# Value products of a cycle over all 512 queries in one PSUM bank, the output job in the other bank

## The chip, the cores and the metric

The kernel runs on one core of one Trainium2 chip. The metric is the device time of one execution in microseconds (us); the kernel before takes 912.35 us, the median of three runs (912.16 to 912.91). Engines are called by the names of the profile: PE is the tensor engine's matrix products and PEld its weight loads, DVE the vector engine, ACT the scalar engine, POOL GpSimd, SP the engine that issues most DMAs.

## The reference, cut to what matters

One attention block and one MLP block read the same x of 2048 tokens by 448 features, and a sigmoid gate per token mixes their results.

```python
q = (x @ wq) in 16 heads of 28;  k = x @ wk;  v = x @ wv      # one key head and one value head for all
p = softmax(q k^T * 28 ** -0.5)
a = (p v of all heads, side by side) @ wo
b = x1 + gelu(layernorm(x1) @ w3) @ w4
out = g * a + (1 - g) * b
```

All is float32. The change lies in `p v`, which the kernel computes together with the scores and the product with `wo`.

## The kernel before, in words

Two stages come first, in the first 400 us of the span: the projections and the token mixing, then the MLP. The third stage is the attention, and all that the change touches is in it. It works through 16 units of 512 queries by 4 heads, and in each unit through 16 tiles of 128 keys. **A cycle** (the loop over `c`, 128 of them, 8 to a unit) takes two key tiles.

PSUM has eight banks of 128 partitions by 512 floats: four `singles` and two `pairs` of two. In cycle `c` the names `s0, s1, s2, s3_` are the four singles, and they change places from cycle to cycle: the banks that are `s0, s1` in one cycle are `s2, s3_` in the next. `pairs[0]` and `pairs[1]` keep their places (after the first cycle, `pair_1` and `pair_0` in the program's own names).

The order of all five engines' instructions is the order in which the code is written, since the schedule is manual. In a cycle the code writes:

1. `score_tiles` (L205) for the first key tile: the transposed scores of four heads, one bank each, in `s0`, `s1` and the two banks of `pairs[0]`. These are three rounds of four products (keys as weights, 32 rows of the array each), and a bank holds its scores after its third product.
2. `exps` (L258) on ACT: the exponential of `s0`, then of `s1`, from PSUM into the tile `p` in SBUF. DVE copies `pairs[0]` into `p` as it is (L953), and ACT does its exponential later, in place.
3. `score_tiles` for the second key tile in `s2`, `s3_` and `pairs[1]`, and `exps` of `s2`, of `s3_`, of `pairs[1]`, and of the copied part of the first tile.
4. `values` (L892): the products of the **preceding** cycle's two `p` tiles with the values. `vext` holds a column of ones beside the 28 value columns, so one product also gives the softmax's sum. Heads stand side by side in the array (32 columns each), and each product is recorded as two. Before the change this is done in two halves of 256 queries: the first half in the left half of `s0`, the second in the left half of `s1`.
5. `values_end` (L813 in a unit's first cycle, L817 in all others) on DVE: adds what stands in PSUM to the unit's sum `o`, once for each half.
6. `run_jobs` or its two parts `job_products` (PE, L843) and `job_adds` (DVE, L859, in the first cycles L878): one **output job**, 224 output columns of 128 tokens of an earlier unit times `wo` (in the first cycles times `w4`), in the right half of `s0`. From cycle 11 on every cycle has a job; before, the odd ones from 3.
7. In the third cycle of a unit (`MAX_AT`), for all units but the last: `max_part` between the two halves, which takes the maxima of the next unit's scores over 16 keys. PE writes them in `pairs[0][:, 0]` (L212), DVE reduces them (L219). There are 15 such cycles. In the last unit a second job stands at that place.

So four banks are used twice in a cycle's length: by a cycle's scores, and by values and job after ACT has read the scores. `s0` and `s1` of a cycle are written next by the second key tile's scores of the next cycle, after DVE has read values and job out of them.

Of the kernel before, what the change touches and what calls it, by code (L numbers as in the profile page):

```python
# [42 lines left out]
def gated_mix_kernel(  # L43
# [152 lines left out]
    def q_low(u):  # L196
        nc.vector.tensor_sub(ql_of[u], qr_of.pop(u), f32(qh_of[u]))
# [24 lines left out]
    def max_part(u, ts, ps):  # L222
        max_products(u, ts, ps)
        max_reduce(u, ts, ps)
# [32 lines left out]
    def exps(p, heads, source=None):  # L257
        nc.scalar.activation(p[:, heads], p[:, heads] if source is None else source, AF.Exp, scale=SCALE)  # L258
# [4 lines left out]
    with tc.tile_pool(name="s1b", bufs=1) as s1b, \  # L263
            tc.tile_pool(name="ps1", bufs=1, space=PSUM) as ps1:
        s1_stack = ExitStack()
        s1 = s1_stack.enter_context(tc.tile_pool(name="s1", bufs=1))
# [55 lines left out]
        def first_queries():  # L322
            ps = [mm1(f"q_{g}") for g in range(NG)]
            ah, al = xact[0]
            cols = [slice(g * P, (g + 1) * P) for g in range(NG)]
            for g in range(NG):
                nc.tensor.matmul(ps[g], wqraw[:, 0, cols[g]], xraw[0][:, 0, :], start=True, stop=False)
            for c in range(1, 4):
                for w, a in ((wqh, ah), (wqh, al), (wql, ah)) if c < 3 else ((wqh, ah), (wql, ah)):
                    for g in range(NG):  # L330
                        nc.tensor.matmul(ps[g], w[:, c, cols[g]], a[:, c, :], start=False, stop=(c == 3 and w is wql))
            return ps
# [160 lines left out]
        q0 = first_queries()  # L493
# [275 lines left out]
    with tc.tile_pool(name="s3", bufs=1, reuse_waits="tile") as s3, \  # L769
# [15 lines left out]
        def q_fetch(u):  # L785
            if u < NU:
                q_load(u, qr)

        def q_begin(u):
            q_high(u, s3.tile([P, 512], F32R, tag="qh", bufs=3, name=f"qh_{u}"),  # L790
                   s3.tile([P, 512], F32R, tag="ql", bufs=3, name=f"ql_{u}"))
# [15 lines left out]
        def values_end(u, pv, qs=slice(0, 512)):  # L807
            if u not in o_of:
                o_of[u] = s3.tile([P, 512], F32, tag="o", bufs=2, name=f"o_{u}")
                fresh.add(u)  # L810
            o = o_of[u][:, qs]
            if u in fresh:
                nc.vector.tensor_copy(o, pv)  # L813
                if qs.stop == 512:
                    fresh.remove(u)
            else:
                nc.vector.tensor_add(o, o, pv)  # L817

        def sums_begin(u):
            o = o_of.pop(u)  # L820
            rt = s3.tile([P, 16], F32, tag="rt", bufs=2, name=f"rt_{u}")
            nc.sync.dma_start(rt, o[0:128:32, :].rearrange("j (a b) -> j a b", b=16))
            return u, o, rt

        def recip(u, o, rt, checked=True):
            rr = s3.tile([P, 16], F32, tag="rr", bufs=2, name=f"rr_{u}")
            nc.vector.reciprocal(rr, rt)
            if checked:
                check(rr.rearrange("p (a b) -> p a b", b=4), 0)
            rd = dram.tile([4, 512], F32, tag="rd", bufs=2, name=f"rd_{u}")  # L830
            nc.sync.dma_start(rd.rearrange("j (a b) -> (j a) b", b=16), rr)
            rb = s3.tile([P, 512], F32, tag="rb", bufs=2, name=f"rb_{u}")
            nc.sync.dma_start(rb, rd.unsqueeze(1).broadcast_to([4, 32, 512]))
            return u, o, rb

        def norm(u, o, rb):
            on_of[u] = s3.tile([P, 512], F32, tag="on", bufs=2, name=f"on_{u}")
            nc.vector.tensor_mul(on_of[u], o, rb)
# [44 lines left out]
        def score_tiles(u, kt, first, second, third, fourth):  # L883
            scores(u, kt, [first, second, third, fourth])
            p_of[u * NT + kt] = p = s3.tile([P, 4, 512], F32, tag="p", bufs=PB, name=f"p_{u}_{kt}")
            return p

        def values(ks, pv, qs=slice(0, 512)):
            for k in ks:
                u, kt = divmod(k, NT)  # L890
                for j in range(4):
                    nc.tensor.matmul(pv[32 * j:32 * j + 32, :], vext[:, kt, :], p_of[k][:, j, qs],  # L892
                                     start=(k == ks[0]), stop=(k == ks[-1]), tile_position=(0, 32 * j))
                if qs.stop == 512:
                    p_of.pop(k)
# [7 lines left out]
        def job_products(ps, n):  # L903
            adds = []
            for _ in range(min(n, len(jobs))):
                products, add, args, cols = jobs.pop(0)
                part = ps[:, 0:D // 2] if n == 1 else ps[:, cols]
                products(*args, part, cols)
                adds.append((add, args, part, cols))
            return adds  # L910

        def job_adds(adds):
            for add, args, part, cols in adds:
                add(*args, part, cols)

        def run_jobs(ps, n):
            job_adds(job_products(ps, n))
# [3 lines left out]
        IDLE = range(2, 12, 2)  # L921
        HINTS = {8 * NT // 2 + 4: [mybir.EngineType.SP],
                 14 * NT // 2 - 2: [mybir.EngineType.DVE, mybir.EngineType.Activation]}
        for c in range(NC):
            u, i = divmod(c, NT // 2)
            k = 2 * c
            s0, s1, s2, s3_ = singles if c % 2 == 0 else singles[2:] + singles[:2]
            if c == 0:
                pb = score_tiles(u, 1, s2, s3_, s0, s1)
                for j, ps in enumerate((s2, s3_, s0, s1)):  # L930
                    exps(pb, slice(j, j + 1), ps.unsqueeze(1))
                pa = score_tiles(u, 2, *(q[:, h] for q in pairs for h in range(2)))
                nc.vector.tensor_copy(pa[:, front], pairs[0])
                for ps, n in zip((s2, s3_), JOBS_0):
                    run_jobs(ps, n)
                exps(pa, both, pairs[1])
                exps(pa, front)
                pairs.reverse()
                continue
            if c > 1:  # L940
                pa = score_tiles(u, 2 * i, s0, s1, pairs[0][:, 0], pairs[0][:, 1])
                with tc.block() if c in HINTS else nullcontext():
                    if c in HINTS:
                        tc.mark_branch_hint_location("redo", "LikelyTaken", HINTS[c])
                    exps(pa, left, s0.unsqueeze(1))
                exps(pa, right, s1.unsqueeze(1))
            if i == 2 and u == 0:
                q_begin(1)
            if i == 3 and u == 0:
                q_low(1)  # L950
                q_fetch(2)
            if 1 < c < NC - 1:
                nc.vector.tensor_copy(pa[:, both], pairs[0])  # L953
            elif c > 1:
                exps(pa, both, pairs[0])
            if i == 3 and later:
                later.pop(0)()
            if i == 1 and sums:
                norms.append(recip(*sums.pop()))
            if i == (3 if u == NU - 1 else 4) and norms:  # L960
                w = norms[0][0]
                norm(*norms.pop())
            if i == 5 and u + 2 < NU:
                q_begin(u + 2)
            if i == 6 and u + 2 < NU:
                q_low(u + 2)
                q_fetch(u + 3)
            pb = score_tiles(u, 2 * i + 1, s2, s3_, pairs[1][:, 0], pairs[1][:, 1])
            exps(pb, left, s2.unsqueeze(1))
            exps(pb, right, s3_.unsqueeze(1))  # L970
            exps(pb, both, pairs[1])
            if 1 < c < NC - 1:
                exps(pa, both)
            if u and i == (3 if u == NU - 1 else 4):
                jobs += [(wo_products, wo_add, (u - 1, t), cols) for t in range(4) for cols in halves]
            v = (c - 1) // (NT // 2)
            at_max = i == MAX_AT and u + 1 < NU
            q0, q1 = slice(0, 256), slice(256, 512)
            values((k - 2, k - 1), s0[:, q0], q0)
            values_end(v, s0[:, q0], q0)  # L980
            if at_max:
                max_part(u + 1, range(4), pairs[0][:, 0])
                later.append(lambda u=u: max_end(u + 1))
            elif i == MAX_AT:
                run_jobs(pairs[0][:, 0], 1)
            values((k - 2, k - 1), s1[:, q0], q1)
            adds = job_products(s0[:, q1], 0 if c in IDLE or c == 1 else 1)
            values_end(v, s1[:, q0], q1)
            job_adds(adds)
            if i == 0 and v < NU - 1:  # L990
                sums.append(sums_begin(v))
        assert not sums and not norms and not later and len(jobs) == 3
# [151 lines left out]
```

## Time and profile before

| what | before |
|---|---|
| median of 3 runs | 912.35 us |
| the profiled execution: its time, its span | 912.95 us, 911.2 us |
| PE busy | 904.7 us (99%) |
| ACT busy | 633.1 us (69%) |
| DVE busy | 517.1 us (57%) |
| granted TensorE clock, mean of the span | 1.000 |
| DMA, mean over the span | 52 GB/s |

The span runs from the first to the last instruction of the program; the execution's own time has 1.75 us more. Matrix products are pipelined: a product's record lasts longer than it keeps the next one waiting, and records of the four heads lie on one another. So PE's busy share says that something was always under way and not that no time is lost. In the views by time a row is a start, a duration, the engine, the line, the operation, out<-in by the program's names with their shape, a count, and in brackets the idle time of the engine before it with what ended it.

### The profile page before, as it was taken

To read this page: it belongs to the slowest core of one execution; us is meant where nothing else is said; L and a number is where in the kernel's file an instruction comes from. 1 tells how busy PE (TensorE), PEld (TensorE's weight loads), DVE (VectorE), ACT (ScalarE), POOL (GpSimd) and SP (SyncE) were. 2 spreads that over 40 slices of the span, in tenths; PEclk is the share of its full clock that TensorE was granted. 3 is DMA by queue.
4 is the path that set the end of the run, shared out by engine and by line. 5 is a ranking of instruction groups with operands and counts; after the bars stand their busy time and mean duration, and the time that the engine had idled before them with its cause. 6 is when DMAs were issued, how large, how long until landed. Compare 5 with 4: busy or idle time off the path is not lost.

```text
span 911.2 us, 24150 instructions
## 1 busy us (share of the span) xinstructions
PE 904.7 (99%) x10360; PEld 627.6 (69%) x10360; DVE 517.1 (57%) x961; ACT 633.1 (69%) x1003; POOL 78.3 (9%) x116
## 2 busy tenths in 40 slices
PE   9999999999999999999999999999999999999998
PEld 6788888888888888875555555555555555555554
DVE  4665273631431531136766776776767667767665
ACT  5442344332131231269999999999999999999995
POOL 3243330200000520020000000000000000000000
PEclk9999999999999999999999999999999999999999
DMA  8832654120110020010000001000011000010001
GB/s 306 282 97 54 150 168 131 32 75 1 35 53 2 18 69 1 1 52 24 14 25 14 24 15 55 23 25 17 24 33 36 25 14 25 15 55 13 15 14 44
DMA packets 40582, 47.31 MB, mean 52 GB/s; under 512 B 10136, under 2 KB 28632, under 8 KB 40472
## 3 DMA queue, kind: packets, MB, share of 16 engines
q1 hardware_dynamic: 37304, 40.30, 15.1%
q10 hardware_dynamic: 3168, 5.44, 1.6%
q8 instruction: 82, 1.34, 0.6%
q14 instruction: 28, 0.23, 0.1%
HBM read 32.56 MB, written 11.67 MB: 49 GB/s over the span
## 4 chain that ended last, share of the span: by engine, by line
PE 98%; ACT 2%; DVE 0%; issue 0%
PE bank L892 26%; PE bank L205 19%; PE bank L843 6%; PE acc L700 5%; PE acc L698 5%; PE acc L699 5%; PE g L137 4%; PE g L138 4%; PE g L136 4%; PE pair L205 3%; ACT p L258 2%; PE hs L474 1%; PE hs L475 1%; PE g L139 1%; PE g L140 1%; PE h L137 1%
## 5 line engine op out<-in xcount | busy, mean ns | idle before, releaser
L258 ACT ACTIVATE p<-bank 128x512 f32<-128x512 f32 x514 | 266.1, 605 | 4.7 <-POOL pick L865 1.5
L892 PE MATMUL bank<-p,vext 128*32 128x256 f32 x4064 | 247.7, 382 | 1.0 <-ACT p L258 0.8
L892 PEld LDWEIGHTS bank<-p,vext 128*32 128x32 f32 x4064 | 118.0, 110 | 115.8 <-ACT p L258 53.0
L953 DVE COPY p<-pair 128x1024 f32<-128x1024 f32 x125 | 153.1, 1225 | 57.2 <-PE pair L205 33.0
L688 ACT ACTIVATE gh<-g 128x512 fp32r<-128x512 f32 x55 | 32.9, 598 | 182.8 <-PE g L140 182.8
L817 DVE TENSOR_TENSOR o<-o,bank 128x256 f32<-128x256 f32 x222 | 93.6, 421 | 81.4 <-PE bank L892 70.3
L258 ACT ACTIVATE p<-p 128x1024 f32<-128x1024 f32 x126 | 138.0, 1095 | 0.0
L258 ACT ACTIVATE p<-pair 128x1024 f32<-128x1024 f32 x129 | 136.7, 1060 | 0.0
L690 DVE TENSOR_TENSOR gl<-gf,gh 128x512 fp32r<-128x512 f32 x55 | 38.5, 699 | 165.8 <-ACT gf L689 165.8
L205 PE MATMUL bank<-qh,kh 32*128 32x512 f32 x514 | 115.2, 444 | 0.1
L205 PE MATMUL pair<-qh,kh 32*128 32x512 f32 x510 | 114.1, 444 | 0.0
L205 PE MATMUL bank<-qh,kl 32*128 32x512 f32 x514 | 102.0, 389 | 0.0
L205 PE MATMUL bank<-ql,kh 32*128 32x512 f32 x514 | 101.8, 390 | 0.0
L205 PE MATMUL pair<-qh,kl 32*128 32x512 f32 x510 | 101.1, 389 | 0.0
L205 PE MATMUL pair<-ql,kh 32*128 32x512 f32 x510 | 100.7, 390 | 0.0
L205 PEld LDWEIGHTS bank<-qh,kh 32*128 32x128 f32 x514 | 48.0, 182 | 62.0 <-issue 38.7
L700 PE MATMUL acc<-w4h,gl 128*128 128x448 f32 x220 | 80.7, 367 | 0.0
L698 PE MATMUL acc<-w4h,gh 128*128 128x448 f32 x220 | 80.2, 365 | 0.0
L699 PE MATMUL acc<-w4l,gh 128*128 128x448 f32 x220 | 79.9, 363 | 0.0
L843 PE MATMUL bank<-wof,on 128*32 128x224 f32 (+1 forms) x984 | 69.5, 357 | 0.0
L136 PE MATMUL g<-ah,w3h 128*128 128x512 f32 x168 | 65.5, 390 | 0.0
L137 PE MATMUL g<-al,w3h 128*128 128x512 f32 x168 | 65.4, 390 | 0.0
(207 smaller groups left out, 1397.5 us busy)
## 6 DMA issues: line engine op xcount, KB each, us to landing
qd<-qf ACTq DMA_DIRECT2D x15, 256.0 KB
rb<-rd SPq DMA_DIRECT2D x15, 256.0 KB
x<-in_x_dram SPq DMA_DIRECT2D x4, 896.0 KB
xd<-xt SPq DMA_DIRECT2D x16, 224.0 KB
w34raw<-in_w_dram SPq DMA_DIRECT2D x7, 512.0 KB
qr<-qd SPq DMA_DIRECT2D x64, 56.0 KB
w34raw<-in_w_dram SPq DMA_DIRECT2D x7, 448.0 KB
out_dram<-ot SPq DMA_DIRECT2D x14, 224.0 KB
```

Of the source, the lines that this page charges most:

```text
L136: nc.tensor.matmul(ps, wh[:, c, :], ah[:, c, :], start=(c == 0), stop=False)
L137: nc.tensor.matmul(ps, wh[:, c, :], al[:, c, :], start=False, stop=False)
L205: nc.tensor.matmul(ps[j], k[h, keys], q[h, :], start=(r == 0), stop=(r == 2), tile_position=(32 * j, 0))
L258: nc.scalar.activation(p[:, heads], p[:, heads] if source is None else source, AF.Exp, scale=SCALE)
L690: nc.vector.tensor_sub(gl, gf, f32(gh))
L698: nc.tensor.matmul(ps, gh[:, tok], w4h[i][:, k, :], start=(f == 0), stop=False)
L699: nc.tensor.matmul(ps, gh[:, tok], w4l[i][:, k, :], start=False, stop=False)
L700: nc.tensor.matmul(ps, gl[:, tok], w4h[i][:, k, :], start=False, stop=(f == stop))
L817: nc.vector.tensor_add(o, o, pv)
L843: nc.tensor.matmul(ps[32 * i:32 * i + 32, :], a[:, c:c + 32], w, start=start, stop=stop, tile_position=(0, 32 * i))
L892: nc.tensor.matmul(pv[32 * j:32 * j + 32, :], vext[:, kt, :], p_of[k][:, j, qs], start=(k == ks[0]), stop=(k == ks[-1]), tile_position=(0, ...
L953: nc.vector.tensor_copy(pa[:, both], pairs[0])
```

## The change

```diff
-            q0, q1 = slice(0, 256), slice(256, 512)
-            values((k - 2, k - 1), s0[:, q0], q0)
-            values_end(v, s0[:, q0], q0)
+            values((k - 2, k - 1), s0)
+            values_end(v, s0)
             if at_max:
                 max_part(u + 1, range(4), pairs[0][:, 0])
                 later.append(lambda u=u: max_end(u + 1))
             elif i == MAX_AT:
                 run_jobs(pairs[0][:, 0], 1)
-            values((k - 2, k - 1), s1[:, q0], q1)
-            adds = job_products(s0[:, q1], 0 if c in IDLE or c == 1 else 1)
-            values_end(v, s1[:, q0], q1)
-            job_adds(adds)
+            run_jobs(s1, 0 if c in IDLE or c == 1 else 1)
```

All 512 queries' value products go to `s0` in products of 512 columns, half as many as before; DVE adds them to `o` in one instruction of 512 columns; the job's products go to the left of `s1`; the maxima stand behind all of the value products. `values` and `values_end` have 512 queries as their default. Lines behind the change are numbered 4 lower in the changed kernel.

PE, the end of a cycle in the 13th unit, before. `bank_0` and `bank_1` are `s0` and `s1` here, `p_...` the exponentials; a row stands for one instruction or several of the same kind (x3, x4), and in brackets are the engines whose semaphores it waits for:

```order
L892 MATMUL bank_0_3209<-p_12_10_9579,vext_78 32x256 [waits Activation_49]
L892 MATMUL bank_0_3209<-p_12_10_9579,vext_78 32x256 x3
L892 MATMUL bank_0_3209<-p_12_11_9598,vext_78 32x256 x4
L892 MATMUL bank_1_3210<-p_12_10_9579,vext_78 32x256 [waits Activation_49]
L892 MATMUL bank_1_3210<-p_12_10_9579,vext_78 32x256 x3
L892 MATMUL bank_1_3210<-p_12_11_9598,vext_78 32x256 x4
L843 MATMUL bank_0_3209<-wof_3256,on_11_9525 32x224 [waits DVE_49]
L843 MATMUL bank_0_3209<-wof_3256,on_11_9525 32x224 x3
L205 MATMUL bank_2_3211<-qh_12_8583,kh_1048 128x512 [waits Activation_49]
```

The same place on PE in the changed kernel:

```order
L892 MATMUL bank_0_3209<-p_12_10_8679,vext_78 32x512 [waits Activation_49]
L892 MATMUL bank_0_3209<-p_12_10_8679,vext_78 32x512 x3
L892 MATMUL bank_0_3209<-p_12_11_8698,vext_78 32x512 x4
L843 MATMUL bank_1_3210<-wof_3256,on_11_8634 32x224 [waits Activation_49]
L843 MATMUL bank_1_3210<-wof_3256,on_11_8634 32x224 x3
L205 MATMUL bank_2_3211<-qh_12_7827,kh_1048 128x512 [waits Activation_49]
```

Sixteen products of 256 columns became eight of 512, and the job's wait for DVE became one for ACT.

PE, the second key tile's scores of the cycle after that, before; these are the next writers of `bank_0` and `bank_1`:

```order
L205 MATMUL bank_0_3209<-qh_12_8583,kh_1048 128x512 [waits DVE_49]
L205 MATMUL bank_1_3210<-qh_12_8583,kh_1048 128x512
L205 MATMUL pair_0_3258<-qh_12_8583,kh_1048 128x512 [waits Activation_49]
L205 MATMUL pair_0_3258<-qh_12_8583,kh_1048 128x512
L205 MATMUL bank_0_3209<-ql_12_8584,kh_1048 128x512
```

The same place on PE in the changed kernel:

```order
L205 MATMUL bank_0_3209<-qh_12_7827,kh_1048 128x512 [waits DVE_49]
L205 MATMUL bank_1_3210<-qh_12_7827,kh_1048 128x512 [waits DVE_49]
L205 MATMUL pair_0_3258<-qh_12_7827,kh_1048 128x512 [waits Activation_49]
L205 MATMUL pair_0_3258<-qh_12_7827,kh_1048 128x512
L205 MATMUL bank_0_3209<-ql_12_7828,kh_1048 128x512
```

The last reader of these banks on DVE, the job's add, read `bank_0` before and reads `bank_1` now, so the wait for it moved from the first product of the four to the second.

DVE, a cycle with maxima in the 14th unit, before; `mr_14` takes the maxima of the next unit out of `pair_1`:

```order
L953 COPY p_13_4_9881<-pair_1_3259 128x1024 [waits PE_49]
L817 TENSOR_TENSOR o_13_9852<-o_13_9852,bank_0_3209 128x256 [waits DVE_49,PE_49,Activation_49]
L219 TENSOR_REDUCE mr_14_9927<-pair_1_3259 128x4x4 [waits PE_49]
L817 TENSOR_TENSOR o_13_9852<-o_13_9852,bank_1_3210 128x256 [waits DVE_49,PE_49,Activation_49]
L859 SCALAR_TENSOR_TENSOR ot_11_8438<-bank_0_3209,gg_79,ot_11_8438 128x224 [waits PE_49]
```

The same place on DVE in the changed kernel:

```order
L953 COPY p_13_4_8936<-pair_1_3259 128x1024 [waits PE_49]
L817 TENSOR_TENSOR o_13_8916<-o_13_8916,bank_0_3209 128x512 [waits DVE_49,PE_49,Activation_49]
L219 TENSOR_REDUCE mr_14_8982<-pair_1_3259 128x4x4 [waits PE_49]
L859 SCALAR_TENSOR_TENSOR ot_11_7700<-bank_1_3210,gg_79,ot_11_7700 128x224 [waits PE_49,Activation_49]
L953 COPY p_13_6_9001<-pair_1_3259 128x1024 [waits PE_49]
```

The reduction stood behind the add of the first half and ahead of that of the second; now it stands behind the add of all 512 queries.

## The prediction

> **What bounds the kernel now.** The page first, to see which engines could be the bound; then the attention stage by itself in the view of windows, as the page's shares are a mean over three stages.
>
> ```profile
> PE 904.7 (99%) x10360; PEld 627.6 (69%) x10360; DVE 517.1 (57%) x961; ACT 633.1 (69%) x1003; POOL 78.3 (9%) x116
> 600.00:700.00 100.00, 100.00 (x1696) 56.73 (x1688) 70.98 (x136) 99.70 (x154) 0.00 (x0) 1.00 0.08 26
> ```
>
> In the 100 us from 600 to 700 PE is busy for 100.00 and ACT for 99.70, at a clock of 1.00; DVE has 29 us to spare. A busy share doesn't tell which of the two sets the pace, so the timeline of one cycle is next: weight loads, then DVE and ACT, then two rows of products.
>
> ```profile
> 603.07 1.45 PEld L892 LDWEIGHTS bank<-p,vext 128*32 128x32 f32 x32 [0.42 <-ACT p L258]
> 605.32 0.18 PEld L205 LDWEIGHTS bank<-qh,kh 32*128 32x128 f32 x2 [0.36 <-issue]
> 605.97 0.19 PEld L205 LDWEIGHTS bank<-qh,kh 32*128 32x128 f32 x2
> 606.96 1.45 PEld L892 LDWEIGHTS bank<-p,vext 128*32 128x32 f32 x32 [0.42 <-ACT p L258]
> 605.13 0.42 DVE L817 TENSOR_TENSOR o<-o,bank 128x256 f32<-128x256 f32 x1 [0.44 <-PE bank L892]
> 605.47 0.45 DVE L859 SCALAR_TENSOR_TENSOR ot<-bank,gg,ot 128x224 f32<-128x224 f32 x1
> 606.31 2.07 ACT L258 ACTIVATE p<-bank 128x512 f32<-128x512 f32 x4
> 606.59 0.38 PE L205 MATMUL pair<-qh,kl 32*128 32x512 f32 x1
> ```
>
> I count from the first value product (603.07). The next cycle's value products start at 606.96, so **a cycle takes 3.89**. The first key tile's scores start at 2.25, the second's at 2.90, the last score product at 3.52. The exponential of `s0` starts at 3.24, and the values, which overwrite `s0`, wait for its end (the bracket). On DVE the second half's add starts at 2.06, the job's add at 2.40, ending at 2.85. Then comes the row that matters: the second tile's scores load weights at 2.90, 0.05 after the job's add. They write the bank that this add reads, so **they already stand right behind DVE**.
>
> That ACT isn't the floor shows in the first cycles, which have a job only every other time (ACT's first exponential of three successive cycles):
>
> ```profile
> 415.13 2.07 ACT L258 ACTIVATE p<-bank 128x512 f32<-128x512 f32 x4
> 418.90 2.10 ACT L258 ACTIVATE p<-bank 128x512 f32<-128x512 f32 x4
> 422.83 2.06 ACT L258 ACTIVATE p<-bank 128x512 f32<-128x512 f32 x4
> ```
>
> 3.77 without a job, 3.93 with one: ACT can do 3.77 and is held to 3.89 by the loop through PE. So up to 0.12 a cycle could be won, and every delay of PE's loop is paid.
>
> One cycle of this execution shows that loop with DVE late (PEld, DVE, PE):
>
> ```profile
> 559.74 1.45 PEld L892 LDWEIGHTS bank<-p,vext 128*32 128x32 f32 x32 [0.41 <-ACT p L258]
> 562.18 0.42 DVE L813 COPY o<-bank 128x256 f32<-128x256 f32 x1 [0.81 <-PE bank L843]
> 562.52 0.44 DVE L859 SCALAR_TENSOR_TENSOR ot<-bank,gg,ot 128x224 f32<-128x224 f32 x1
> 563.02 0.18 PEld L205 LDWEIGHTS bank<-qh,kh 32*128 32x128 f32 x2 [0.49 <-DVE ot L859]
> 563.60 0.41 PE L205 MATMUL pair<-qh,kl 32*128 32x512 f32 x2
> 563.93 0.16 PEld L892 LDWEIGHTS bank<-p,vext 128*32 128x32 f32 x8 [0.37 <-ACT p L258]
> ```
>
> Here DVE's add came 0.38 later than usual (2.44). The job's add ended at 3.22, the scores' weights followed at 3.28 with DVE named as releaser, and the values 0.91 behind them: 4.19, which is 0.30 longer than usual. In such a cycle ACT's exponential is long done. The price is nearly the delay itself, because there was next to no slack.
>
> **The change, part by part.**
>
> *Value products.* Sixteen of 256 columns become eight of 512. What a column costs, from rows of two widths: the last group of four at 256 is followed by the next group 0.22 later, groups of 448 follow each other in 0.38.
>
> ```profile
> 608.50 0.40 PE L892 MATMUL bank<-p,vext 128*32 128x256 f32 x4
> 608.72 0.56 PE L843 MATMUL bank<-wof,on 128*32 128x224 f32 x8
> 903.98 0.56 PE L843 MATMUL bank<-wof,on 128*32 128x448 f32 x4
> 904.36 0.56 PE L843 MATMUL bank<-wof,on 128*32 128x448 f32 x4
> ```
>
> That is 0.86 and 0.85 ns a column, the same within the rounding: nothing to win by width, at most 0.01 a cycle, and the values end where they ended. TensorE: Matmul & The Clock Gate of the Trainium skill, section Back-to-back issue gap, gives 81 ns for a sustained product of 128 columns and 131 ns for one of 512, less than half per column; by an estimate from these two, value products would shrink by far more than the whole 0.12 that ACT leaves open. The rows above show no such saving.
>
> *The job.* It no longer waits for DVE. That wait (18.5 us of PEld in all, its row is with the rivals) hid behind products: the job's first one (608.72) follows the values' last group (608.50) in a group's usual 0.22. Worth nothing.
>
> *The add.* One instruction in place of two. Rows for its length (DVE, by operation and shape):
>
> ```profile
> L817 DVE TENSOR_TENSOR o<-o,bank 128x256 f32<-128x256 f32 x222 | 93.6, 421 | 81.4 <-PE bank L892 70.3 <-ACT p L258 7.3 <-issue 2.7
> L764 DVE TENSOR_TENSOR x<-x,acc 128x448 f32<-128x448 f32 x4 | 2.4, 622 | 7.2 <-PE acc L700 7.2
> L838 DVE TENSOR_TENSOR on<-o,rb 128x512 f32<-128x512 f32 x15 | 10.2, 681 | 0.0
> ```
>
> 421 ns at 256 and 622 at 448 make 1.047 ns a column, so 0.69 at 512; below stands 0.68 (no operand in PSUM), above twice 0.42. DVE saves time in sum. But before, half of it was done while PE was still at the second half; only 0.42 lay behind the last product. Now all 0.69 does.
>
> *The loop.* The add starts at 2.05. The next instruction on DVE starts 0.08 before an add's end (605.13 + 0.42 against 605.47): the job's add at 2.66, ending at 3.11. Its bank is now `s1`, so the second product of the second tile's scores waits for it, and all behind that one: weights at 3.16. Values 0.91 behind, as in the late cycle: 4.07. **Against 3.89 that is 0.18 a cycle.** Ends: 4.02 if the loads of the other heads, made meanwhile, save the array's filling; 4.12 with the usual cycle's 0.99 between these weights and the values (2.90 to 3.89). Cycles with a job and scores behind it, none of the dear kind below and not the late one: 101 from 11 to 126, and 3, 5, 7, 9: 105. **18.9 us**, ends 13.7 and 24.2. The cycles without a job have ACT's 3.77 as their floor, and the single add frees `s0` at 2.74; I cost them at nothing.
>
> *Cycles with maxima.* Rows of one (PE, DVE, PEld):
>
> ```profile
> 626.42 1.07 PE L892 MATMUL bank<-p,vext 128*32 128x256 f32 x16
> 627.30 0.30 PE L212 MATMUL pair<-khd,qh 128*32 128x64 bf16 x16
> 627.95 0.42 DVE L219 TENSOR_REDUCE mr<-pair 128x16 f32<-128x256 f32 x1
> 628.78 0.19 PEld L205 LDWEIGHTS bank<-qh,kh 32*128 32x128 f32 x2 [0.36 <-ACT p L258]
> 630.43 0.59 PEld L892 LDWEIGHTS bank<-p,vext 128*32 128x32 f32 x16 [0.42 <-ACT p L258]
> ```
>
> 4.01 a cycle, 0.12 above the others for the extra products. The reduction ends at 1.95, and the next cycle's first scores, which write the same pair, load at 2.36: 0.41 of cover. In the changed order the reduction stands behind the long add: 2.66 to 3.08. The third product of the **first** key tile's scores waits for it, to 3.13, and everything on PE behind. From those scores to the values PE alone needs 1.27 (605.32 to 606.59) and 0.33 (563.60 to 563.93), 1.60 in all: 4.73, 0.72 more. Ends: 4.53, if the two heads that don't wait run ahead and only ACT counts, and 4.77 with the usual 1.64 (605.32 to 606.96). The last unit's extra job, DVE's 0.45 on the same pair, I cost alike: 16 cycles, **11.5 us**, ends 8.3 and 12.2.
>
> *The sum:* 18.9 + 11.5 = 30.4 us on the profiled execution's 912.95 (span 911.2 and 1.75 around it): 943.3. That execution lies 0.60 above the median of the runs, so I predict **942.7 us**; by the ends 934.4 to 948.8.
>
> **The rivals.**
>
> *Freed products (faster).* One mechanism: the value products and the job get through PE earlier, because wide products are cheaper and no job waits for an add. It decides only if PE gives back time that DVE's longer add doesn't take, over 0.18 a cycle. ACT's 3.77 is then the floor: 105 x 0.12 = 12.6 us, 899.8. For it: the weight loads of the job did wait.
>
> ```profile
> L843 PEld LDWEIGHTS bank<-wof,on 128*32 128x32 f32 x896 | 24.1, 108 | 24.3 <-DVE o L817 18.5 <-DVE o L813 3.3
> ```
>
> Those are 21.8 us of waits for DVE from 450 to 890 us. Against it: the products' rows without a gap, and the same price per column. PSUM — Partial Sum Buffer of the Trainium skill, section PSUM bank collisions raise a hardware error, wants two engines kept apart by whole bank and 32 partitions, not by address; by that rule the old job had to wait for the add of the other columns, and the trace agrees (18.5 us). The page doesn't say that such a wait costs time.
>
> *Cover in ordinary cycles.* The second tile's scores have more slack than the late cycle shows, so that only cycles with maxima pay: 912.35 + 11.5 = 923.9. Against it: 0.05 from add to weights in the usual cycle, and 0.30 lost for 0.38.
>
> *The change does nothing.* Both waits are taken up by a slack in ACT that I don't see: 912. Against it: 3.89 is already above ACT's 3.77.
>
> *A dearer add.* If 512 columns take twice 0.42, the loop grows by 0.15 more in all 121 cycles: 18.2 us, 960.9. Against it: 622 ns at 448.
>
> **How the numbers follow.** Forecast 0.82; cover in ordinary cycles 0.07; dearer add 0.05; freed products 0.03; nothing 0.03. 912.35 within 0.2% (1.8 us) is about what a measurement can't tell from no change. Faster 0.03, same 0.03, slower 0.94. The range takes in the ends and a little for what the 0.05 steps between engines may do: 932 to 951; cover, freed products, nothing and the dearer add lie outside with 0.18.
>
> **What would show it.** In the changed profile: values starting 4.07 apart in ordinary cycles and 4.7 in those with maxima; the weight loads of the second tile's scores waiting for DVE's job add, some 0.3 each time; the third load of the first tile's scores waiting for the reduction in 15 cycles; ACT's share from 600 to 700 us falling from 99.7 to about 93; the 512-column add at 0.69. The prediction is wrong if those loads wait no longer than now, if the values end earlier than 1.9 after their start, or if ACT stays at 99.7.

## The result and the profile after

The changed kernel takes **941.5 us**, the median of four runs (940.93 to 942.86), against 912.3 us before (also four runs by now): a ratio of 1.0319 with a 95% interval of 1.0307 to 1.0331. The profiled execution took 941.43 us, its span is 939.6 us, so the profiled executions differ by 28.5 us and their spans by 28.4 us.

The page's first part, and the window from 600 to 700 us of the changed kernel:

```profile
PE 929.0 (99%) x8328; PEld 583.4 (62%) x8328; DVE 499.9 (53%) x834; ACT 636.3 (68%) x1003; POOL 79.9 (8%) x116
600.00:700.00 100.00, 99.17 (x1213) 45.48 (x1209) 63.98 (x104) 94.79 (x145) 0.00 (x0) 1.00 0.07 22
```

DVE has 17 us less to do and PEld 44 us, and the kernel is 29 us slower. In the window DVE's share fell from 71 to 64 and so did ACT's, from 99.7 to 94.8: ACT, which was nearly full, now waits. PE still reads 99, since a product's record lasts longer than it keeps the next one waiting (0.40 against 0.22 in the prediction's rows at 608.50 and 608.72); a busy share of PE wouldn't have shown the loss.

An ordinary cycle, weight loads first, then DVE and ACT:

```profile
626.57 0.16 PEld L892 LDWEIGHTS bank<-p,vext 128*32 128x32 f32 x8 [0.36 <-ACT p L258]
628.80 0.18 PEld L205 LDWEIGHTS bank<-qh,kh 32*128 32x128 f32 x2 [0.36 <-ACT p L258]
629.37 0.18 PEld L205 LDWEIGHTS bank<-qh,kh 32*128 32x128 f32 x1
629.72 0.18 PEld L205 LDWEIGHTS bank<-qh,kh 32*128 32x128 f32 x1 [0.17 <-DVE ot L859]
630.62 0.16 PEld L892 LDWEIGHTS bank<-p,vext 128*32 128x32 f32 x8 [0.37 <-ACT p L258]
628.62 0.69 DVE L817 TENSOR_TENSOR o<-o,bank 128x512 f32<-128x512 f32 x1 [1.58 <-PE bank L892]
629.22 0.45 DVE L859 SCALAR_TENSOR_TENSOR ot<-bank,gg,ot 128x224 f32<-128x224 f32 x1
629.80 1.58 ACT L258 ACTIVATE p<-bank 128x512 f32<-128x512 f32 x3
```

Counted from the first value product, the add starts at 2.05 and the job's add at 2.65; it ends at 3.10. The first of the second tile's loads is made at 2.80 and the next only at 3.15, 0.05 behind the job's add, with DVE named in the bracket. The values follow 0.90 later: the cycle is 4.05 long. The last load's bracket names ACT, but ACT's exponential of `s0` started at 629.80 and takes 0.6, so it was done at 630.40, 0.22 ahead. What the values wait for is PE's own scores in front of them: the last of these start at 630.29, 0.33 ahead, as far as in the late cycle of the prediction. That is the sign that PE's loop is no longer held by ACT, as it was before.

A cycle with maxima:

```profile
638.74 0.16 PEld L892 LDWEIGHTS bank<-p,vext 128*32 128x32 f32 x8 [0.37 <-ACT p L258]
641.09 0.18 PEld L205 LDWEIGHTS bank<-qh,kh 32*128 32x128 f32 x2 [0.36 <-ACT p L258]
641.86 0.18 PEld L205 LDWEIGHTS pair<-qh,kh 32*128 32x128 f32 x2 [0.59 <-DVE mr L219]
643.46 0.16 PEld L892 LDWEIGHTS bank<-p,vext 128*32 128x32 f32 x8 [0.36 <-ACT p L258]
640.79 0.69 DVE L817 TENSOR_TENSOR o<-o,bank 128x512 f32<-128x512 f32 x1 [1.59 <-PE bank L892]
641.39 0.42 DVE L219 TENSOR_REDUCE mr<-pair 128x16 f32<-128x256 f32 x1
642.66 1.09 ACT L258 ACTIVATE p<-bank 128x512 f32<-128x512 f32 x2 [0.84 <-PE bank L205]
```

The first two heads of the first tile's scores load at 2.35, the other two at 3.12, behind the reduction that stands behind the long add. ACT idles 0.84 for scores. The cycle is 4.72 long.

The view of waits from 450 us on (who waited for whom, us in total, times, the longest) has both places, and ACT's wait in the cycles with maxima:

```profile
PEld bank L205 <- DVE ot L859: 16.9, 100, 0.3
ACT p L258 <- PE bank L205: 11.9, 15, 0.8
PEld pair L205 <- DVE mr L219: 7.7, 13, 0.6
```

Before, from 440 to 890 us, the first had 3 waits and 1.2 us, the second one wait and 0.3 us, and the third didn't appear. The totals of PEld are idle time of a weight load, which is less than what a wait costs the loop, since loads run ahead of products: the one made at 629.37 above belongs to a product that starts at 629.60.

### The profile page after: what moved, and what is told of

The parts are those of the page before. It is cut to its first block, busy times and chain, and to the rows that moved or that the text cites. A ratio compares the mean times of both kernels' runs of the same rounds, so it can differ in the third digit from the quotient of the medians.

```text
span 939.6 us, 20078 instructions
## 1 busy us (share of the span) xinstructions
PE 929.0 (99%) x8328; PEld 583.4 (62%) x8328; DVE 499.9 (53%) x834; ACT 636.3 (68%) x1003; POOL 79.9 (8%) x116
## 4 chain that ended last, share of the span: by engine, by line
PE 97%; DVE 2%; issue 1%; ACT 0%; DVEq 0%
PE bank L892 25%; PE bank L205 20%; PE acc L700 5%; PE bank L843 5%; PE acc L698 5%; PE acc L699 5%; PE pair L205 4%; PE g L136 4%; PE g L138 4%; PE g L137 4%; PE hs L474 1%; PE hs L475 1%; PE g L139 1%; PE g L140 1%; PE h L137 1%; PE h L136 1%
## 5 line engine op out<-in xcount | busy, mean ns | idle before, releaser
L892 PE MATMUL bank<-p,vext 128*32 128x512 f32 x2032 | 244.3, 598 | 0.0
L817 DVE TENSOR_TENSOR o<-o,bank 128x512 f32<-128x512 f32 x111 | 76.4, 688 | 144.0 <-PE bank L892 93.5
L205 PE MATMUL bank<-qh,kh 32*128 32x512 f32 x514 | 138.5, 466 | 0.0
L205 PE MATMUL pair<-qh,kh 32*128 32x512 f32 x510 | 125.0, 488 | 5.0 <-DVE mr L219 4.9
L892 PEld LDWEIGHTS bank<-p,vext 128*32 128x32 f32 x2032 | 53.0, 109 | 122.6 <-issue 76.0
L205 PE MATMUL bank<-ql,kh 32*128 32x512 f32 x514 | 126.3, 398 | 0.0
L205 PE MATMUL bank<-qh,kl 32*128 32x512 f32 x514 | 123.8, 389 | 0.0
L205 PEld LDWEIGHTS bank<-qh,kh 32*128 32x128 f32 x514 | 66.4, 182 | 71.1 <-ACT p L258 44.9
L205 PEld LDWEIGHTS bank<-qh,kl 32*128 32x128 f32 x514 | 67.0, 183 | 7.6
L843 PEld LDWEIGHTS bank<-wof,on 128*32 128x32 f32 x984 | 30.7, 110 | 63.1 <-issue 32.2
```

Source lines behind the costliest of these rows:

```text
L205: nc.tensor.matmul(ps[j], k[h, keys], q[h, :], start=(r == 0), stop=(r == 2), tile_position=(32 * j, 0))
L843: nc.tensor.matmul(ps[32 * i:32 * i + 32, :], a[:, c:c + 32], w, start=start, stop=stop, tile_position=(0, 32 * i))
```

## The experiments

All are set against the kernel before on the same chip; each median is of four executions, e7's of ten. "Loop theory" is that of the prediction: the time from the last value product to the end of DVE's last reading of the banks decides when the next scores may start. The cycle lengths are the distances between the first value loads of successive cycles in the profile.

### e1: add only half the columns

```diff
-                nc.vector.tensor_add(o, o, pv)
+                h = slice(0, 256)
+                nc.vector.tensor_add(o[:, h], o[:, h], pv[:, h])
```

> The changed kernel, but in all cycles of a unit except its first DVE adds only the first 256 of the 512 columns of value products to the sum (the other half of the queries' sums stays without them: part of the computation is left out). PE's program is the same. Loop theory (what stands on DVE behind the last value product, the add and then the job's add, sets when the next cycle's second scores may start): the job's add ends at 2.85 instead of 3.10 after the first value product, the loop through PE and ACT takes over at 3.89, so 90 ordinary cycles fall from 4.06 to about 3.88 (15 cycles that copy 512 columns stay), 16 cycles with maxima or a second job from 4.71 to 4.46: about 921.9 us. Rival (the wide products in one bank, or the job's other bank, cost time on PE by themselves): cycles stay at 4.06, 941 us.

Measured: 921.01 us (920.76 to 921.14), ratio to before 1.0094 (1.0077 to 1.0111). One cycle (DVE, PEld):

```profile
651.83 0.42 DVE L818 TENSOR_TENSOR o<-o,bank 128x256 f32<-128x256 f32 x1 [1.40 <-PE bank L893]
652.23 0.45 DVE L860 SCALAR_TENSOR_TENSOR ot<-bank,gg,ot 128x224 f32<-128x224 f32 x1
649.78 0.16 PEld L893 LDWEIGHTS bank<-p,vext 128*32 128x32 f32 x8 [0.40 <-ACT p L258]
652.59 0.32 PEld L205 LDWEIGHTS bank<-qh,kh 32*128 32x128 f32 x2
653.67 0.16 PEld L893 LDWEIGHTS bank<-p,vext 128*32 128x32 f32 x8 [0.40 <-ACT p L258]
```

The same products of 512 columns stand in the same bank and the job in the same other bank, and the cycle is 3.89 again; the second tile's loads start without an idle row. The 15 cycles that still copy 512 columns stay at 4.06, those with maxima are at 4.45; these two kinds are why the time is still 9 us above that before. So neither width nor banks cost the time; the columns on DVE do.

### e2: narrow products, one bank

```diff
-            values((k - 2, k - 1), s0)
+            for q in (slice(0, 256), slice(256, 512)):
+                values((k - 2, k - 1), s0[:, q], q)
```

> The changed kernel, but its value products are 16 of 256 columns again, both halves in the same bank; the single add and the job's bank stay. Loop theory: width is worth at most 0.01 us a cycle, cycles 4.06 to 4.07, 941 to 943 us. Rival (products of 512 columns are dearer or cheaper than two of 256): several us off, below 938 if wide products are what costs, above 946 if they save something that the longer add hides.

Measured: 942.34 us (942.03 to 943.14), 0.8 us more than the changed kernel, with runs that overlap its runs; ordinary cycles 4.066 against 4.058. Half as many products are worth 0.008 us a cycle.

### e3: two adds of 256 columns

```diff
-            values_end(v, s0)
+            for q in (slice(0, 256), slice(256, 512)):
+                values_end(v, s0[:, q], q)
```

> The changed kernel, but DVE adds the 512 columns in two instructions of 256, both behind the last value product. Loop theory: two instructions take 0.34 + 0.34 to the job's add where one takes 0.61, so 0.07 a cycle more in 105 ordinary and 16 dear cycles: cycles of 4.13 and 4.78, 950 us. Rival (only the bank and the width matter, not when DVE is done): 941 us.

Measured: 948.5 us (948.07 to 951.04), ratio 1.0395 (1.0377 to 1.0412); ordinary cycles 4.114, those with maxima 4.78. On DVE:

```profile
653.41 0.75 DVE L817 TENSOR_TENSOR o<-o,bank 128x256 f32<-128x256 f32 x2 [1.04 <-ACT p L258]
654.08 0.45 DVE L859 SCALAR_TENSOR_TENSOR ot<-bank,gg,ot 128x224 f32<-128x224 f32 x1
651.36 0.16 PEld L892 LDWEIGHTS bank<-p,vext 128*32 128x32 f32 x8 [0.37 <-ACT p L258]
655.47 0.13 PEld L892 LDWEIGHTS bank<-p,vext 128*32 128x32 f32 x4 [0.37 <-ACT p L258]
```

This profile is that of the slowest of the four executions, and 1.8 us of what it has more than the changed kernel's lie behind the last value products. The two adds stand merged in one row (x2). From the start of the first to the job's add 0.67 pass, against 0.60 with a single one: 0.06 to 0.07 a cycle more, as the cycles have it. The single add as such is the better one, once both halves end together. Its forecast of 950 was 1.5 us high, since 0.07 was taken where 0.056 came.

### e4: maxima between the key tiles

```diff
-            values((k - 2, k - 1), s0)
-            values_end(v, s0)
             if at_max:
+                values((k - 2, k - 1), s0, n=1)
                 max_part(u + 1, range(4), pairs[0][:, 0])
                 later.append(lambda u=u: max_end(u + 1))
-            elif i == MAX_AT:
+                values((k - 2, k - 1), s0, n=2)
+            else:
+                values((k - 2, k - 1), s0)
+            values_end(v, s0)
+            if i == MAX_AT and not at_max:
                 run_jobs(pairs[0][:, 0], 1)
```

Here `n` picks the first or the second key tile of the two; its lines in `values` are left out here.

> The changed kernel, but in the 15 cycles with maxima their products stand between the value products of the first and of the second key tile, so that DVE reduces them while PE is still at values. Loop theory with a second term for these cycles (the first scores wait for the reduction behind the long add): they fall from 4.71 to 4.06 + 0.12 = 4.18, 8 us in all: 933.4 us, ordinary cycles unchanged at 4.06. Rival (the 15 cycles are long for another reason, the maxima's products or the next unit's queries): no change, 941 us.

Measured: 931.72 us (931.3 to 932.57), ratio 1.0215 (1.0198 to 1.0232), 9.8 us less than the changed kernel. A cycle with maxima:

```profile
667.19 0.43 DVE L219 TENSOR_REDUCE mr<-pair 128x16 f32<-128x256 f32 x1 [0.87 <-PE pair L212]
668.02 0.69 DVE L817 TENSOR_TENSOR o<-o,bank 128x512 f32<-128x512 f32 x1 [0.40 <-ACT p L258]
665.85 0.16 PEld L892 LDWEIGHTS bank<-p,vext 128*32 128x32 f32 x8 [0.36 <-ACT p L258]
668.20 0.19 PEld L205 LDWEIGHTS bank<-qh,kh 32*128 32x128 f32 x2 [0.36 <-ACT p L258]
670.01 0.16 PEld L892 LDWEIGHTS bank<-p,vext 128*32 128x32 f32 x8 [0.36 <-ACT p L258]
```

4.16 instead of 4.72, ordinary cycles unchanged at 4.06. The second term is shown: 13 cycles by 0.55 are 7.1 us, and the two in the first units, now 3.99 and 3.81 for 4.72 and 4.71, add 1.6; that makes 8.8, for 8 expected. The remaining 1.0 us has nothing to do with the edit: the first value product of the attention starts at 403.06 in this profile and at 404.04 in that of the changed kernel.

### e5: the kernel before with DVE late

```diff
             values_end(v, s1[:, q0], q1)
+            if adds:
+                nc.vector.tensor_add(extra_out, extra_in, extra_in)
             job_adds(adds)
```

The two tiles, and the fill of `extra_in` ahead of the attention, are left out here.

> The kernel before, with one more DVE instruction, a sum of 180 columns in SBUF that nobody reads, between the second half's add and the job's add in every cycle with a job; it delays the job's add by about 0.27 us and touches no PSUM. Loop theory: ordinary cycles go from 3.89 to 4.06 as with the change, though not one product, bank or add of the kernel before is altered, and the cycles with maxima, whose reduction stays in its place, only from 4.01 to 4.20: about 932.6 us. Rival (DVE has 29 us to spare in 100, so an instruction more is hidden; the change's cost lies in PE's products): 912 us.

Measured: 931.63 us (931.37 to 932.12), ratio 1.0205 (1.0188 to 1.0222). One cycle:

```profile
652.35 0.42 DVE L821 TENSOR_TENSOR o<-o,bank 128x256 f32<-128x256 f32 x1 [0.44 <-PE bank L896]
652.69 0.34 DVE L994 TENSOR_TENSOR extra_out<-extra_in 128x180 f32<-128x180 f32 x1
652.95 0.44 DVE L863 SCALAR_TENSOR_TENSOR ot<-bank,gg,ot 128x224 f32<-128x224 f32 x1
650.29 1.45 PEld L896 LDWEIGHTS bank<-p,vext 128*32 128x32 f32 x32 [0.37 <-ACT p L258]
653.44 0.18 PEld L205 LDWEIGHTS bank<-qh,kh 32*128 32x128 f32 x2 [0.37 <-DVE ot L863]
654.34 0.16 PEld L896 LDWEIGHTS bank<-p,vext 128*32 128x32 f32 x8 [0.36 <-ACT p L258]
```

An instruction that reads and writes nothing of use, 0.26 long to the next one's start, makes the old kernel's ordinary cycle 4.05, nearly the changed kernel's 4.06, with 16 products of 256 columns in two banks. Cycles with maxima go to 4.17 only, since the reduction kept its place.

### e6: the job's add first

```diff
-            values_end(v, s0)
             if at_max:
...
             run_jobs(s1, 0 if c in IDLE or c == 1 else 1)
+            values_end(v, s0)
```

> The changed kernel, but with the job's add ahead of the values' add on DVE: the same instructions in another order, the same banks. Loop theory: the job's products end at 2.30, so its add runs from 2.40 to 2.85 and the values' add from 2.77 to 3.46; the next second scores load at 3.51 and the values follow 0.91 behind, 4.42 in 105 ordinary cycles (4.06 now), and 4.52 in those with maxima (4.71 now): about 976 us. Rival (what counts is how much DVE and PE have to do, not in which order): 941 us.

Measured: 979.07 us (978.67 to 979.49), ratio 1.0722 (1.0704 to 1.074). One cycle:

```profile
648.70 0.45 DVE L859 SCALAR_TENSOR_TENSOR ot<-bank,gg,ot 128x224 f32<-128x224 f32 x1 [2.27 <-PE bank L843]
649.09 0.69 DVE L817 TENSOR_TENSOR o<-o,bank 128x512 f32<-128x512 f32 x1
646.26 0.16 PEld L892 LDWEIGHTS bank<-p,vext 128*32 128x32 f32 x8 [0.36 <-ACT p L258]
649.83 0.18 PEld L205 LDWEIGHTS bank<-qh,kh 32*128 32x128 f32 x2 [0.80 <-DVE o L817]
650.73 0.16 PEld L892 LDWEIGHTS bank<-p,vext 128*32 128x32 f32 x8 [0.36 <-ACT p L258]
```

The same instructions in another order on DVE, and 37.6 us more: DVE now stands idle until the job's products end, and the long add comes last. A typical cycle is 4.44 (4.47 here), for 4.42 expected; those with maxima are 4.57, for 4.52.

### e7: both repairs

> The changed kernel with both repairs: maxima between the key tiles, and only the first 256 of 512 columns added in all cycles of a unit except its first (part of the computation is left out). Loop theory: ordinary cycles 3.88, those with maxima 4.00, the cycle with a second job 4.46, 15 cycles that copy 512 columns 4.06: about 915 us, that is, the two terms together hold nearly the whole loss of 29 us. Rival (a third cause): well above 918 us.

The edits are those of e1 and e4. Measured: 914.04 us (913.13 to 915.71), ratio 1.0014 (1.0004 to 1.0023). The window from 600 to 700 us:

```profile
600.00:700.00 100.00, 100.00 (x1285) 47.61 (x1280) 62.72 (x109) 99.19 (x154) 0.00 (x0) 1.00 0.08 26
```

ACT is full again. With half of the columns off DVE and the maxima early, wide products in one bank and the job in the other run within 0.14% of the kernel before. No third cause of any size is left: the upper end of the interval, 1.0023, is 2 us. (Half of the sum isn't added here, so this is a measurement and not a version to use.)

No run points to a version that beats the kernel before: with the loop through DVE shortened as in e7, PE and ACT hold the cycle at 3.88, where they held it before.

## Why the prediction was right

The forecast was 942.7 us, the time is 941.5. Its terms, against the cycles of the two profiles (after less before, added up over the cycles of each kind):

| term | forecast | measured |
|---|---|---|
| ordinary cycles with a job | 18.9 | 17.3 |
| 15 cycles with maxima and the one with a second job | 11.5 | 11.6 |
| three cycles without a job | 0 | -0.3 |
| all | 30.4 | 28.5 |

*Value products.* Right: worth nothing. The values end where they ended, the add starts at 2.06 before and at 2.05 now, and e2 puts the width at 0.008 us a cycle. The sustained figures in the section Back-to-back issue gap of the page TensorE: Matmul & The Clock Gate of the Trainium skill, by which wide products would have been much cheaper per column, don't hold for these products.

*The job.* Right: the wait for DVE that it lost gave nothing; e7, which doesn't have it either, is no faster than the kernel before.

*The add.* Right: 0.69 long, 688 ns in the mean of 111.

```profile
L817 DVE TENSOR_TENSOR o<-o,bank 128x512 f32<-128x512 f32 x111 | 76.4, 688 | 144.0 <-PE bank L892 93.5
```

*The loop.* Right in place and kind, 0.013 a cycle too long: 4.058 measured, 4.07 forecast. From the waiting load to the values 0.90 pass, for 0.91 taken from the late cycle, and the job's add ends at 3.10 instead of 3.11. The load of the first head, made ahead at 2.80, saved almost nothing, so the lower end (4.02) wasn't reached. The job's add ends 0.25 later than before, and the cycle is 0.168 longer: the rest was the slack of the values, which used to start 0.99 behind those loads and now start 0.90 behind. The upper end has an error of addition: 3.16 and 0.99 make 4.15 and not 4.12, which would put the upper end of the time at 952 instead of 948.8. The lower ends 4.02 and 4.53 were given without a working.

*Maxima.* Right: 4.72 for 4.73. That the heads which don't wait run ahead didn't help, as taken. The two such cycles in the first units cost more, 1.0 and 0.9, and the one with a second job less, 0.47, than the 0.72 that I took for all.

*Cycles without a job.* Costed at nothing; they became 0.11 shorter each (3.81 to 3.70). Before, ACT's work left over from the cycle ahead held them. That cycle is longer now, so ACT has caught up: the values of the 4th, the 6th and the 8th cycle start 0.18 to 0.23 behind the end of ACT's exponential of `s0`, where they started 0.05 behind. ACT itself still takes 3.77 to 3.78 from such a cycle to the next, so that floor was right.

*The rivals.* Freed products fell with e2, and with ACT at 94.8 in the window. Cover in ordinary cycles fell with the 100 waits for the job's add, and with e5. A change that does nothing fell with the time. The dearer add fell with the 0.69; even two instructions for one, in e3, cost 948.5 and not 960.9.

*The signs.* Two were off in size: the loads that wait for the job's add idle for 0.17 each and not for some 0.3, since the first head's load goes ahead of them, and ACT's share fell to 94.8 and not to 93.

## What to carry to other kernels

When two engines take turns on the same banks, count what stands behind the last product until the bank is free, not the sum of the work. Two halves, of which one is evicted while the other is computed, can be faster than one instruction that costs less in all; here 17 us less of DVE made 29 us more. A load that starts within a few hundredths of its releaser's end is such a place, even if its idle time in the view of waits is near nothing, and one disturbed cycle in the profile can show its price beforehand.

## What I had not expected of the hardware

In each profile of these runs one to four ordinary cycles are late by 0.08 or more for no reason that the schedule gives: before, the 41st and the 108th by 0.30 and 0.26, after, the 9th and the 87th by 0.18 and 0.13. They take 0.2 us off the difference. The places go with DVE's program. In e1, e2, e4 and e7, where DVE has as many records in the trace as in the changed kernel (1242, waits for semaphores included), the same 9th and 87th cycles are late; in e3, e5 and e6, which have other numbers of them, other cycles are. In each of them one DVE instruction starts late, the copy in the 41st by 0.38. Counted over these records, the late instructions are numbers 704 and 1216 before, 448 and 960 after, 576 in e3 and e6, and 576, 704, 832 and 1344 in e5: all are 64 more than a multiple of 128. Not every such number makes a cycle late, and what happens there is not shown.
